# Down-projection by seven products of quarters (Strassen's kind), with running sums in PSUM, and a new order of all work

## The chip, the cores and the metric

One core of a Trainium2 chip runs the kernel. The metric is the device time of one execution, in microseconds. TensorE (PE) multiplies matrices from SBUF into PSUM, which has eight banks; VectorE (DVE) and ScalarE (ACT) can read PSUM; GpSimd (POOL) cannot, and it also issues DMAs, as SyncE (SP) does.

## The reference

A recurrent attention (decay per head) is followed by a normalised, gated feed-forward layer without biases. Cut to what matters:

```python
batch, n_heads, seq, head_dim = 4, 8, 768, 64      # 3072 tokens, d_model 512, d_ff 1536
for t in range(S):
    state = gamma * state + k_t (outer) v_t        # per batch and head
    y[t] = scale * q_t @ state
x = y as (B*S, H*D)
xn = x / sqrt(mean(x*x) + 1e-6) * rms_g
out = (silu(xn @ w_gate) * (xn @ w_val)) @ w_out   # float32 out
```

The last product is the down-projection: 3072 x 1536 by 1536 x 512.

## The kernel before

The 768 positions are cut into six chunks c of 128; with the four batches b a chunk has 512 tokens. For each (c, b) the attention computes masked scores (A, then M0 and M1 on VectorE write am), the output y (Y, in PSUM), the state update (K, U, B), the sum of squares (S, ScalarE), the reciprocal root (R, GpSimd), the normalised rows xn (N, VectorE) and their transpose xnT (X and XE on engines for chunks 0 and 1, a transposing DMA from SP later). Inputs come through L (Lq, Lk, Lv; @P is GpSimd's queue, which casts to bf16 on the way, @S is SP's, in float32), are cast or scaled by Ck, Cq and V, and transposed by Tq/Tk with copies Eq/Ek (chunks 0 and 1) or by DMA (tq, tk). J and D make decayed keys for chunks 0 and 1.

The feed-forward layer works on a chunk. Its 1536 inner columns are 12 slices n of 128. `g.c.n0.n1.b0.b1` and `v...` multiply slices of w_gate and w_val by xnT into a bank each (L549: four matmuls of 128x128 by 128x512 for a slice with all four batches), `s` is Silu on ScalarE (L559), `h` multiplies both on VectorE into the activations hT (L567). The down-projection `d.c.b.n0.n1` (L574) has, for each batch, 12 matmuls of a 128x128 slice of hT, held as weights, by 128x512 of w_out; `o` copies the bank out (L146, a helper for all copies), `st` stores it (L587). The last tile of the last chunk, (5, 3), is done by `e` in three pieces of 192, 192 and 128 columns (L596), so that the last copy and store are small. hT is a ring of two tiles of 12 slices, o_sb a ring of four.

All instructions stand in an order written out by hand in the string ORDER: each word names a function, its arguments, after `/` the PSUM banks, after `@` the engine. Every engine runs its own instructions in this order and waits by semaphores for others. The weights arrive by GpSimd DMAs (wg.n0.n1, wv.n0.n1, wo.n0.n1) placed among its other work. H and hot are filler matmuls on a constant, whose result nobody reads (L240, L234).

The functions that the diff touches are printed here.

Of the kernel before, what the change touches and what calls it, by code (L numbers as in the profile page):

```python
# [9 lines left out]
F32 = mybir.dt.float32  # L10
BF16 = mybir.dt.bfloat16
# [6 lines left out]
H.8/3 yt Lk.0.2@S ident Ck.0.2@D vd Lk.1.1@S iota Tk.0.2/0 rms.1@S D.0.2@D Lk.0.0@P Lq.0.1@P H.3/1 Tk.0.0/2  # L18
H.1/1 Tq.0.1/7 Ek.0.0@D mk1 hot.3/1 J.0.0/3 D.0.0@D mk0 Lq.0.0@P Lk.0.1@P Tq.0.0/6 Lq.0.2@P Eq.0.1@A Eq.0.0@A
Tk.0.1/5 Ek.0.1@A Ek.0.2@D yd Lk.0.3@P H.1/1 Tq.0.2/4 tab Lq.0.3@P Eq.0.2@D hot.2/0 A.0.0/5017 M0.0.0 G/2 M1.0.0  # L20
Tq.0.3/6 Lv.0.0@P M0.0.1 GE@A Tk.0.3/3 Eq.0.3@A Lv.0.1@P M1.0.1 Lv.0.2@P Lv.0.3@P wg.0.2 Y.0.0/4 wv.0.2 A.0.2/21
wg.2.4 M1.0.2 Ek.0.3@A Lq.1.1@P H.3/0 A.0.3/61 S.0.0 M0.0.2 H.1/0 Y.0.2/3 K.0.0/0 J.0.1/5 M1.0.3 R.0.0 S.0.2
N.0.0 M0.0.3 Y.0.1/1 H.1/2 X.0.0/4 J.0.3/7 wv.2.4 S.0.1 XE.0.0@D U.0.0@A R.0.2 R.0.1 Ck.1.1@A N.0.2 B.0.0 H.2/2
Y.0.3/0 g.0.0.2.0.1/2 K.0.2/6 S.0.3 s.0.0.2.0.1 N.0.1 U.0.2@A wg.4.6 X.0.2/4 R.0.3 XE.0.2@D D.0.1@D
v.0.0.2.0.1/3 X.0.1/2 wv.4.6 causal XE.0.1@A Lk.1.2@P v.0.0.2.2.3/4 wg.6.9 Lq.1.2@P wv.6.9 h.0.0.2.0.1
g.0.0.2.2.3/6 D.0.3@D Lq.1.0@P g.0.0.2.1.2/5 g.0.2.3.0.3/3 s.0.0.2.2.3 h.0.0.2.2.3 s.0.0.2.1.2 g.0.3.4.0.3/6
N.0.3 v.0.0.2.1.2/4 D.1.1@D Tq.1.1/5 Lk.1.0@P Tk.1.1/0 X.0.3/7 Eq.1.1@D K.0.1/2 wg.9.12 v.0.3.4.0.3/1 Lv.1.1@P
s.0.3.4.0.3 XE.0.3@A g.0.0.4.3.4/6 s.0.2.3.0.3 h.0.0.2.1.2 g.0.4.6.3.4/4 wv.9.12 g.0.4.5.0.3/7 v.0.4.6.3.4/5
v.0.2.3.0.3/3 U.0.1@D s.0.4.6.3.4 Ek.1.1@A h.0.3.4.0.3 g.0.5.6.0.3/0 s.0.4.5.0.3 h.0.4.6.3.4 mc.0@P mc.1@P
v.0.4.5.0.3/5 v.0.0.4.3.4/7 h.0.2.3.0.3 Tk.1.2/1 g.0.6.7.0.4/4 Ek.1.2@A Lv.1.2@P h.0.4.5.0.3 g.0.7.8.0.4/2  # L30
Lv.1.0@P wo.0.4 Tq.1.2/1 s.0.5.6.0.3 s.0.7.8.0.4 Eq.1.2@D B.0.1 g.0.8.9.0.4/3 A.1.2/51 v.0.5.6.0.3/0 M1.1.2
wo.4.8 wo.8.12 s.0.0.4.3.4 v.0.7.8.0.4/2 h.0.0.4.3.4 h.0.5.6.0.3 h.0.7.8.0.4 Lk.1.3@P D.1.2@P Lk.2.0@S
v.0.6.7.0.4/7 Tk.1.0/0 M0.1.2 Lk.2.3@S Tq.1.0/6 v.0.8.9.0.4/1 s.0.6.7.0.4 Ek.1.0@A Eq.1.0@D h.0.6.7.0.4
s.0.8.9.0.4 Lq.2.1@S A.1.0/6042 M0.1.1 M1.1.0 B.0.2 M1.1.1 g.0.11.12.0.4/3 g.0.9.10.0.4/5 g.0.10.11.0.4/4
s.0.11.12.0.4 K.1.1/3 Y.1.1/0 s.0.10.11.0.4 h.0.8.9.0.4 S.1.1 U.1.1@D M0.1.0 v.0.9.10.0.4/2 v.0.10.11.0.4/3
R.1.1 v.0.11.12.0.4/4 s.0.9.10.0.4 K.0.3/7 h.0.9.10.0.4 D.1.0@P U.0.3@A Y.1.2/2 S.1.2 h.0.10.11.0.4 Y.1.0/3
N.1.1 h.0.11.12.0.4 Lq.1.3@P S.1.0 B.0.3 Lq.2.0@S Lk.2.1@S K.1.0/7 X.1.1/5 R.1.2 K.1.2/1 U.1.2@D d.0.3.0.4/0
N.1.2 R.1.0 N.1.0 d.0.0.0.4/6 XE.1.1@D d.0.1.0.4/4 d.0.2.0.4/2 X.1.0/5 d.0.3.4.8 X.1.2/1 d.0.0.4.8 Lv.1.3@P
d.0.1.4.8 XE.1.2@D d.0.1.8.12 U.1.0@D XE.1.0@A B.1.1 g.1.0.1.0.3/7 Tk.1.3/5 g.1.1.2.0.3/3 d.0.3.8.12 Tq.1.3/1
o.0.1@D Eq.1.3@D d.0.0.8.12 s.1.1.2.0.3 Ek.1.3@A o.0.3@A A.1.3/13 M1.1.3 Ck.2.0@A M0.1.3 tk.2.0 v.1.1.2.0.3/0  # L40
d.0.2.4.8 o.0.0@A Y.1.3/3 h.1.1.2.0.3 v.1.0.1.0.3/6 Ck.2.3@D S.1.3 R.1.3 Cq.2.1@D g.1.3.4.0.3/1 v.1.2.3.0.3/4
# [24 lines left out]
d.2.2.0.12/1 R.3.3 K.3.2/4 N.3.0 S.3.2 N.3.3 d.2.1.0.10/2 d.2.1.10.12 XE.3.0@S Lq.5.2@S R.3.2 N.3.2 Ck.5.2@D
XE.3.2@S d.2.3.0.12/3 U.3.3@D XE.3.3@S U.3.2@D Lk.4.2@S o.2.2@D Lq.4.2@S Lv.5.3@S U.3.0@D d.2.0.0.10/4 tk.4.0
# [36 lines left out]
def kernel(  # L104
# [43 lines left out]
    def flat(x):  # L148
        return x.rearrange("p h d -> p (h d)")
# [485 lines left out]
```

## Time and profile before

| | |
|---|---|
| time, median of 3 runs | 235.12 us (234.45 to 295.99) |
| the profiled execution | span 233.6 us, 4637 instructions |
| mean granted TensorE clock | 0.993 |
| gate and value products, busy | 70.0 and 71.2 us, 344 matmuls each |
| down-projection, busy | 63.5 us in 276 matmuls of 512 columns, and 36 narrower ones |
| filler matmuls H | 8.5 us in 20 |
| memory traffic | 28.31 MB read, 6.29 MB written, 148 GB/s |

The profile comes from one execution. Its times are from the span's start; "busy" is the time in which an engine had an instruction of the group running, and since matmuls are pipelined and their ends modelled, the mean of one matmul in a group is longer than its share of a stream. "PEld" is the load of the stationary operand, beside PE.

### The profile page before, as it was taken

The numbers are of one execution on the slowest core, as the hardware profiler recorded it, in microseconds if no ns is written. First come the engines' busy times: TensorE is split into PE (matmuls) and PEld (weight loads), VectorE is DVE, ScalarE is ACT, GpSimd is POOL, SyncE is SP. The second block draws the span as 40 slices with busy tenths as digits, with TensorE's granted clock in tenths as the row PEclk, the third lists the DMA queues.
The fourth block names the chain that finished last, engine by engine and source line by source line (L and its number), as shares of the span: only waits on it lengthen the run. The fifth ranks groups of instructions, "written<-read, shape, count | busy, mean of one in ns | idle before, by whom it ended". The sixth has DMA issues, their size and how long they took to land.

```text
span 233.6 us, 4637 instructions
## 1 busy us (share of the span) xinstructions
PE 227.6 (97%) x1771; PEld 120.8 (52%) x1771; DVE 130.4 (56%) x241; ACT 96.1 (41%) x231; POOL 89.7 (38%) x163
## 2 busy tenths in 40 slices
PE   8799999999999999999999999999999999999994
PEld 2458855645545655445554444554455444444444
DVE  6479639753662965628975239866367532323320
ACT  7658433514337231464731346553265332232202
POOL 8958998550544555030273741247003100000000
PEclk9979999999999999999999999999999999999999
DMA  7999999999798888999988899968511400020222
GB/s 126 147 180 123 127 179 184 205 145 215 133 206 214 171 194 140 262 218 221 235 173 146 179 221 206 198 149 142 148 61 27 112 0 0 3 90 9 83 89 93
DMA packets 105353, 33.61 MB, mean 144 GB/s; under 512 B 94449, under 2 KB 102385, under 8 KB 105330
## 3 DMA queue, kind: packets, MB, share of 16 engines
q1 hardware_dynamic: 81858, 25.70, 50.2%
q0 software_dynamic: 23472, 7.60, 30.1%
q8 instruction: 14, 0.23, 0.4%
q14 instruction: 9, 0.07, 0.1%
HBM read 28.31 MB, written 6.29 MB: 148 GB/s over the span
## 4 chain that ended last, share of the span: by engine, by line
PE 89%; DMA 4%; POOL 2%; ACT 2%; DVE 1%; issue 0%; SPq 0%; POOLq 0%; DVEq 0%; ACTq 0%
PE v_ps L549 27%; PE g_ps L549 27%; PE o_ps L574 21%; PE a_ps L403 3%; DMA kb<-in_k_dram 3%; PE y_ps L441 2%; PE kv_ps L526 2%; PE y_ps L445 2%; DMA out_dram<-o_sb 1%; PE o_ps L596 1%; PE hot_ps L240 1%; PE t_ps L366 1%; PE t_ps L371 1%; PE xt_ps L495 1%; ACT xsq L455 1%; ACT xsq L458 1%
## 5 line engine op out<-in xcount | busy, mean ns | idle before, releaser
L567 DVE TENSOR_TENSOR hT<-sg,v_ps 128x512 bf16<-128x512 bf16 (+2 forms) x76 | 48.7, 656 | 47.8 <-PE v_ps L549 34.8
L549 PE MATMUL v_ps<-xnT,wv_b 128*128 128x512 bf16 (+2 forms) x344 | 71.2, 345 | 0.1
L559 ACT ACTIVATE sg<-g_ps 128x512 bf16<-128x512 f32 (+2 forms) x76 | 42.1, 575 | 70.6 <-PE g_ps L549 68.1
L549 PE MATMUL g_ps<-xnT,wg_b 128*128 128x512 bf16 (+2 forms) x344 | 70.0, 344 | 0.0
L574 PE MATMUL o_ps<-wo_b,hT 128*128 128x512 bf16 x276 | 63.5, 379 | 0.0
L549 PEld LDWEIGHTS <-wg_b 128*128 128x128 bf16 x344 | 30.4, 98 | 29.3
L549 PEld LDWEIGHTS <-wv_b 128*128 128x128 bf16 x344 | 30.2, 98 | 28.9 <-DVE am L426 0.6
L574 PEld LDWEIGHTS <-hT 128*128 128x128 bf16 x276 | 26.3, 98 | 29.1
L468 POOL TENSOR_SCALAR ms<-ssq 128x1 f32<-128x1 f32 x24 | 4.6, 190 | 59.1 <-ACT xsq L458 58.4
L426 DVE TENSOR_TENSOR am<-a_ps,causal 128x512 bf16<-128x512 f32 x32 | 20.6, 685 | 7.8 <-PE a_ps L403 7.5
L339 POOL TENSOR_TENSOR qb<-qf,ydec 128x512 bf16<-128x512 f32 x13 | 14.0, 1074 | 25.2 <-DMA qf<-in_q_dram 24.9
L146 ACT COPY o_sb<-o_ps 128x512 f32<-128x512 f32 (+1 forms) x16 | 8.8, 552 | 29.7 <-PE o_ps L574 23.1
L458 ACT ACTIVATE xsq<-y_ps 128x512 f32<-128x512 f32 x22 | 13.2, 599 | 18.9 <-PE y_ps L445 13.7
L482 DVE SCALAR_TENSOR_TENSOR xn<-y_ps,rstd,g_bc 128x512 bf16<-128x512 f32 x22 | 16.3, 748 | 4.3 <-POOL rstd L470 3.0
L146 DVE COPY o_sb<-o_ps 128x512 f32<-128x512 f32 (+1 forms) x10 | 6.4, 648 | 18.1 <-PE o_ps L574 12.2
L541 POOL CAST st_b<-st_f 64x256 bf16<-64x256 f32 x40 | 15.9, 398 | 1.3
L470 POOL TENSOR_TENSOR rstd<-ms,mhalf 128x1 f32<-128x1 f32 x24 | 13.3, 552 | 2.0
L534 DVE TENSOR_TENSOR st_f<-st_f,kv_ps 128x512 f32<-128x512 f32 x16 | 10.8, 684 | 5.2 <-PE kv_ps L526 4.6
L356 ACT ACTIVATE vp<-vf,vdec 128x64 bf16<-128x64 f32 x48 | 12.2, 343 | 0.0
L426 DVE TENSOR_TENSOR am<-a_ps,mask 128x512 bf16<-128x512 f32 x16 | 10.4, 686 | 2.5 <-PE a_ps L403 2.3
L240 PE MATMUL hot_ps<-one 128*128 128x512 bf16 x20 | 8.5, 547 | 1.1 <-DVE one L153 1.1
L441 PEld LDWEIGHTS <-am 128*128 128x128 bf16 x176 | 7.8, 99 | 3.1 <-issue 0.3
(99 smaller groups left out, 174.8 us busy)
## 6 DMA issues: line engine op xcount, KB each, us to landing
out_dram<-o_sb SPq DMA_DIRECT2D x23, 256.0 KB, 2.4
kf<-in_k_dram SPq DMA_DIRECT2D x18, 256.0 KB, 3.8
qf<-in_q_dram SPq DMA_DIRECT2D x16, 256.0 KB, 3.9
vf<-in_v_dram SPq DMA_DIRECT2D x16, 256.0 KB, 3.9
wo_b<-in_moe_w_out_dram POOLq DMA_DIRECT2D x3, 512.0 KB, 12.2
qb<-in_q_dram POOLq DMA_DIRECT2D x8, 128.0 KB, 6.6
vp<-in_v_dram POOLq DMA_DIRECT2D x8, 128.0 KB, 6.5
kb<-in_k_dram POOLq DMA_DIRECT2D x6, 128.0 KB, 5.9
```

The source lines that it names most:

```text
L146: (e.copy if e is ACT else e.tensor_copy)(out, in_)
L339: e.tensor_tensor(out=u["qb"], in0=u["qf"], in1=ydec[:, c, :, None].to_broadcast([128, H, D]), op=ALU.mult)
L426: DVE.tensor_tensor(out=u["am"][:, i], in0=u["a"][i], in1=m, op=ALU.mult)
L441: nc.tensor.matmul(y[:, h, :], u["am"][:, h % 2, h // 2, :], u["vp"][:, h, :], start=h == 0, stop=c == 0 and h == H - 1, skip_group_check= ...
L458: ACT.activation(xsq, flat(u["y"]), AF.Square, accum_out=u["ssq"])
L470: POOL.tensor_tensor(out=u["rstd"], in0=ms, in1=mhalf, op=ALU.pow)
L482: DVE.scalar_tensor_tensor(out=u["xn"], in0=flat(u["y"]), scalar=u["rstd"], in1=g_bc, op0=ALU.mult, op1=ALU.mult)
L541: POOL.tensor_copy(st_b[b][r, :, i * 64:i * 64 + 64], st_f[b][r, :, i * 64:i * 64 + 64])
L549: nc.tensor.matmul(p[:, (n - n0) * m:(n - n0 + 1) * m], W[w][0][:, s, n * 128:(n + 1) * 128], xnT[c][:, s, b0 * C:b1 * C], start=s == 0, s ...
L559: ACT.activation(sg[:, :cols], done["wg", c, n0, b0][:, :cols], AF.Silu)
L567: DVE.tensor_tensor(out=hT[c][:, n0:n1, b0 * C:b1 * C], in0=sg, in1=p, op=ALU.mult)
L574: nc.tensor.matmul(o_ps[c, b], hT[c][:, n, b * C:(b + 1) * C], wo_b[:, n, :], start=n == 0, stop=n == NFF - 1)
```

## The change

Chunk 0 keeps the old down-projection (`d`, `o`, `st`). For chunks 1 to 5 the product hT by w_out is cut into quarters: tokens into two halves of 256 (batches 0, 1 and 2, 3), the inner dimension into two halves (of every four slices, the first two and the last two), the output columns into two halves of 256. Instead of eight products of quarters there are seven, by Winograd's form of Strassen's method. With A11, A12, A21, A22 for the quarters of the activations (first index: half of the tokens) and B for those of w_out:

- w1 = B12 - B11, w2 = B22 - w1, w3 = B22 - B12 (in place of B12), w4 = B21 - w2: once, three on VectorE, w3 on GpSimd, 1536 bf16 elements in each partition.
- z1 = A21 + A22, z2 = z1 - A11, z3 = A11 - A21 (in place of A21), z4 = A12 - z2: for each chunk and each third r of the slices, 512 bf16 elements in each partition: 60 instructions, 33 on VectorE and 27 on GpSimd.
- Products: 1 = A11 B11, 2 = A12 B21, 3 = z4 B22, 4 = A22 w4, 5 = z1 w1, 6 = z2 w2, 7 = z3 w3. Each is 12 matmuls of 128x128 by 128x256 into one bank, which holds two blocks of 128 tokens.
- Bank a takes 1, 6, 7 and 4 as a running sum. After 1, 6 and 7 a copy q leaves it (q1, q6, q7), mostly by ScalarE; after 4 it is the third quarter, C21, copied by r4. Bank b takes 2, and r1 = b + q1 (VectorE) is C11. Bank c takes 5, r2 = c + q7 is C22; then 3 is added into it, and r3 = c + q6 is C12. s1 to s4 store the quarters, 256 KB each.

Word for word in the new order: `a1.c.r0.r1`, `a6`, `a7`, `a4`, `b2`, `c5`, `c3` are the products.

Buffers change with it: hT is a ring of five tiles of four slices; z shares a ring of 12 with kd; w shares three wide tiles with the masks of chunks 0 and 1; the results share o_sb, five tiles, with two tiles of the start; xsq is one bf16 tile. The pieces `e` are gone. The whole ORDER is another one. Its start, the part around the first sums, and its end:

```diff
+Lk.0.2@S rms.1@S Lk.1.1@S Lq.0.3@P Lk.0.0@P Lk.0.1@P Lq.0.0@P H.8/0 H.1/1 Lq.0.1@P iota hot.3/2 mk1 ident yt pick
+Lq.0.2@P Tq.0.3/3 Tk.0.0/4 Ck.0.2@D vd Ck.1.1@A D.0.2@D H.1/5 Lk.0.3@P Lq.1.2@P Tk.0.1/6 Lv.0.0@P Eq.0.3@D Lv.0.1@P
+Tk.0.2/7 Ek.0.2@D Ek.0.0@A Tq.0.0/0 Lk.1.0@P Ek.0.1@A J.0.0/1 D.0.0@D Tq.0.1/2 Eq.0.0@A Tk.1.1/5 Lv.0.2@P Eq.0.1@A
+J.0.1/4 D.0.1@D Ek.1.1@D Tq.0.2/3 A.0.0/6701 M1.0.0 M1.0.1 Eq.0.2@A Tk.0.3/2 mk0 M0.0.1 Ek.0.3@A G/4 M0.0.0 Lk.1.2@P
+Tq.1.2/5 A.0.3/37 M1.0.3 A.0.2/12 Lv.0.3@P M0.0.2 Lk.1.3@P Eq.1.2@D Y.0.1/0 S.0.1 wg.4.6 Lq.1.3@P K.0.0/6 U.0.0@A
+K.0.1/7 Y.0.0/1 hot.2/6 U.0.1@A GE@A M0.0.3 M1.0.2 J.0.3/5 R.0.1 wg.6.9 H.1/7 S.0.0 R.0.0 Y.0.3/6 N.0.1 N.0.0 wv.6.9
+S.0.3 Tk.1.0/2 Tk.1.2/4 Y.0.2/3 H.2/7 Tk.1.3/0 S.0.2 Ek.1.2@A Ek.1.0@D Ek.1.3@A R.0.3 H.3/7 D.0.3@D X.0.1/1 K.0.2/2
+XE.0.1@A N.0.3 R.0.2 K.0.3/4 U.0.3@A wv.4.6 Lq.1.1@P X.0.0/7 A.1.2/50 N.0.2 X.0.3/6 XE.0.3@D XE.0.0@A Tq.1.3/1 X.0.2/4
+XE.0.2@D yd tab U.0.2@A g.0.4.6.3.4/3 g.0.6.7.0.4/7 s.0.4.6.3.4 wg.0.2 Eq.1.3@D g.0.5.6.0.3/6 g.0.7.8.0.4/4
...
+h.1.11.12.0.4 Y.2.1/5 S.2.1 v.1.8.9.0.4/4 R.2.1 N.2.1 s.1.10.11.0.4 d.0.3.8.12 v.1.10.11.0.4/2 A.3.0/3601 Lk.3.2@S
+o.0.3@A h.1.8.9.0.4 Cq.3.3@D V.3.0@P h.1.10.11.0.4 a1.1.0.3/5 M1.3.0 q1.1@D B.2.0 XE.2.0@S K.3.0/7 U.3.0@D B.2.1
+z1.1.2@D M0.3.1 b2.1.0.3/4 XE.2.2@S XE.2.1@S g.2.3.4.0.4/2 v.2.3.4.0.4/6 s.2.3.4.0.4 Lv.3.2@S z2.1.0@D g.2.10.11.0.4/7
...
+Lk.5.3@S Ck.5.3@P P.4.2/451630 B.4.2 N.4.1 q1.2@A M1.4.2 M0.4.3 M0.4.2 a6.2.0.3 M1.4.3 Y.4.0/7 V.5.2@A K.4.3/5
...
+c5.4.0.3/5 h.5.10.11.0.4 z4.5.0@D z1.5.2@D z3.5.2@D r2.4 s3.3@S s2.4@S z4.4.1@D b2.5.0.2/1 a6.5.0.2 b2.5.2.3 r1.5
+z2.5.2@P a6.5.2.3 q6.5@A s1.5@S c5.5.0.2/0 a7.5.0.2 c5.5.2.3 s2.3@S a7.5.2.3 z4.5.2@D z4.4.0@D c3.4.0.3 q7.5@A r2.5
+s2.5@S a4.5.0.2 H.1/7 r3.4 s3.4@S a4.5.2.3.0 z4.5.1@P c3.5.0.2 r4.5.0@A a4.5.2.3.1 s4.5.0@S r4.5.1@A s4.5.1@S c3.5.2.3
+r3.5 s3.5@S H.3/4
```

The code, cut to its core:

```diff
+    HB, OB, KD, SN = 5, 5, 12, 3
+    def wide(name):
+        return sb.tile([128, 1024], F32, name=name, tag="wide", bufs=3)
...
-            hT[c] = ring([128, NFF, GT], BF16, "hT", 2)
+            hT[c, r] = ring([128, 4, GT], BF16, "hT", HB)
...
+    wo_q = wo_b.rearrange("p (r j i) m -> p r j i m", j=2, i=2)
+    def block(j, m):
+        return wo_q[:, :, j, :, m * HM:(m + 1) * HM]
+    def quarter(c, r, i, j):
+        return hT[c, r][:, (J0, J1)[j], (LO, HI)[i]]
+    def zsum(i, e, c, r, x, a, b, how):
+        if x is None:
+            x = sb.tile([128, 2, GT // 2], BF16, name="z", tag="kd", bufs=KD)
+        e.tensor_tensor(out=x, in0=a, in1=b, op=how)
+        done["z", i, c, r] = x
...
+    def product(x, i, bk, c, r0, r1, p=None):
+        first = i in (1, 2, 5) and r0 == 0
+        if first:
+            done[x, c] = bank(bk[0], [128, 2, HM], F32, x)
+        for q in (0, 1) if p is None else (p,):
+            for r in range(r0, r1):
+                for k in (0, 1):
+                    nc.tensor.matmul(done[x, c][:, q], left(i, c, r)[:, k, q * C:q * C + C], right(i)[:, r, k],
+                                     start=first and q == r == k == 0, stop=r == 2 and k == 1, skip_group_check=True)
+    def keep(i, e, c):
+        done["q", i, c] = ring([128, 2, HM], F32, "sn", SN)
+        copy(e, done["q", i, c], done["a", c])
+    QUARTER = {1: ("b", 1, 0, 0), 2: ("c", 7, 1, 1), 3: ("c", 6, 0, 1), 4: ("a", None, 1, 0)}
+    def result(i, e, c, p=None):
...
+            DVE.tensor_tensor(out=done["r", i, c][:, s], in0=done[x, c][:, s], in1=done["q", q, c][:, s], op=ALU.add)
+    def store(i, e, c, p=None):
+        _, _, t0, m = QUARTER[i]
+        s = slice(0, 2) if p is None else slice(p, p + 1)
+        e.dma_start(out=out_v[c][s.start + 2 * t0:s.stop + 2 * t0, :, m * HM:(m + 1) * HM]
+                    .rearrange("b p m -> p b m"), in_=done["r", i, c][:, s])
```

More of the change, by code (lines that the diff above doesn't have):

```diff
@@ L192 @@
     g_bc = const.tile([128, DM], F32, name="g_bc")
-    g_row = const.tile([1, DM], F32, name="g_row")
+    g_row = spare([128, DM], F32, "g_row")[0:1]
     ones = const.tile([1, 128], F32, name="ones")
@@ L584, in st, with o @@
[L584 to L597 removed]
+    def o(e, bk, c, b):
+        done["o", c, b] = ring([128, DM], F32, "o_sb", OB)
+        copy(e, done["o", c, b], o_ps[c, b])
```

226 lines of the change are left out of this document (121 added, 105 removed).

## The prediction

> **What bounds the kernel now.** I read the page's first two parts, then the shares of the chain that ended last.
>
> ```profile
> span 233.6 us, 4637 instructions
> PE 227.6 (97%) x1771; PEld 120.8 (52%) x1771; DVE 130.4 (56%) x241; ACT 96.1 (41%) x231; POOL 89.7 (38%) x163
> PEclk9979999999999999999999999999999999999999
> PE 89%; DMA 4%; POOL 2%; ACT 2%; DVE 1%; issue 0%; SPq 0%; POOLq 0%; DVEq 0%; ACTq 0%
> ```
>
> TensorE is busy 97% of the span, the chain runs through it for 89%, and the clock is full but for one early slice. A busy row does not yet say that it works at its rate, so I took the chain in order of time (columns: start, length, what), where a run of matmuls shows its spacing.
>
> ```profile
> 24.20 0.45 PE t_ps L371 x8
> 53.94 0.65 PE g_ps L549 x4
> 75.41 0.55 PE a_ps L403 x16
> 88.32 2.59 PE o_ps L574 x12
> 227.81 2.66 PE o_ps L596 x36
> 230.50 0.32 ACT o_sb L146
> ```
>
> Per matmul: 0.45 / 8 = 56 ns for 128 columns, 0.65 / 4 = 163 for 384, 2.59 / 12 = 216 for 512. That is a straight line, 0.416 ns a column and about 3 ns on top. TensorE is bound by columns streamed, and only fewer columns, or less waiting, shorten it. Where does it not stream? At the start:
>
> ```profile
> 5.00:19.38 14.38, 12.88 (x218) 7.66 (x217) 9.47 (x16) 10.02 (x25) 10.61 (x18) 0.88 1.56 164
> 19.38 0.61 PE L549 MATMUL g_ps<-xnT,wg_b 128*128 128x128 bf16 x8
> 61.00:131.00 70.00, 70.00 (x513) 36.40 (x512) 43.40 (x71) 28.33 (x73) 29.30 (x51) 1.00 0.94 199
> L240 PE MATMUL hot_ps<-one 128*128 128x512 bf16 x20 | 8.5, 547 | 1.1 <-DVE one L153 1.1
> ```
>
> The stretches are: length, then busy time (count) of PE, PEld, DVE, ACT, POOL, then granted clock and DMA. The first gate product comes at 19.38; until then 20 wide filler matmuls stand in for work. Afterwards TensorE is full (70.00 of 70 from 61 to 131) while VectorE has 43.40 in 71 instructions there, 0.61 each. So after 19 us a saved column is a saved time, as long as no other engine fills up.
>
> **The products.** Chunks 1 to 5 used 48 matmuls of 512 columns each; the last chunk used 36 and the 36 narrow ones of L596. Before: 4 x 48 x 0.2158 + 36 x 0.2158 + 2.66 = 51.86 us. Now a chunk has seven products of 3 x 2 x 2 = 12 matmuls with 256 columns: 84 a chunk, 420 in all. No 256-column matmul is in the trace; the line gives 256 x 0.416 + 3 = 109 ns, between the rows of 128 and 384 columns. What could spoil it is the load of the stationary operand, of which there are now 420 for 240 (and 36):
>
> ```profile
> L574 PEld LDWEIGHTS <-hT 128*128 128x128 bf16 x276 | 26.3, 98 | 29.1
> ```
>
> One takes 98 ns, less than 109, and behind 128-column matmuls loads of this length keep a pitch of 56, so they overlap. Bounds: 109 and, if a load of 98 hid only half, 158. I take 109: 420 x 0.1092 = 45.89, a gain of **5.97 us**.
>
> A rule speaks against this split: the Trainium skill ("TensorE: Matmul & The Clock Gate", Back-to-back issue gap) gives 81 ns for 128 columns and 131 for 512 in streams of load and matmul, so about half of a wide matmul would be a fixed price. An estimate from that page, 98 ns for 256, would make the change 420 x 98 - 240 x 131 ns = 9.7 us dearer. The trace disagrees at both ends, with 56 and 216 ns.
>
> **What the other engines get.** Rows of the groups by shape (count, busy us and mean ns):
>
> ```profile
> L146 ACT COPY o_sb<-o_ps 128x512 f32<-128x512 f32 x14 | 8.2, 586 | 28.0 <-PE o_ps L574 23.1 <-DMA out_dram<-o_sb 4.8
> L146 DVE COPY o_sb<-o_ps 128x512 f32<-128x512 f32 x9 | 6.1, 687 | 14.6 <-PE o_ps L574 12.2 <-DMA out_dram<-o_sb 2.4
> L517 DVE TENSOR_TENSOR kd<-kb,vdec 128x512 bf16<-128x512 bf16 x3 | 2.1, 686 | 0.3 <-ACT vdec L259 0.3
> L146 DVE COPY xnT<-xt_ps 128x512 bf16<-128x512 bf16 x5 | 2.1, 422 | 2.1 <-PE xt_ps L495 2.1
> L517 POOL TENSOR_TENSOR kd<-kb,vdec 128x512 bf16<-128x512 bf16 x2 | 2.1, 1035 | 0.1
> 11.61 2.48 DVE L426 TENSOR_TENSOR am<-a_ps,mask 128x512 bf16<-128x512 f32 x4
> ```
>
> Removed: 22 of the 26 copies of o. Added: 15 sums r1 to r3 on VectorE, 15 mid copies q and 6 copies r4, mostly on ScalarE, where 586 each about equals the 16 copies that leave it. Further 60 sums z (33 on VectorE, 27 on GpSimd) and four sums w of three times the width. A z has 512 bf16 elements and two SBUF operands, which the trace shows only with a broadcast factor in another type (686); the bf16 copy's 422 is the other bound. I take 422, since nothing in a z is wider than bf16, and keep 686 for the range. GpSimd: 27 x 1.04 + 3.1 (w3) = 31 us on 89.7, free enough.
>
> VectorE must be judged by stage. Between the call z1.1.0 and the first product of chunk 3 the new order has 97 VectorE instructions beside 65 us of matmuls (the order's matmuls at the pitches above). Of these 15 (z and casts) cost 0.42, three w 1.2 each, and 79 cost 0.62, the pitch of the four masks in a row (2.48 / 4): 6.3 + 3.6 + 49.0 = 58.9 of 65, 91%; with z at the upper price 61.5. Before it was 43.40 of 70, 62%. TensorE is still the longer, so I cost all this at **nothing**, and TensorE's work is the cover: 6.1 us of room. When it is used up, the next late thing is a PSUM bank that VectorE has not emptied.
>
> **New waits.** After products 1, 6 and 7 a copy q must leave the bank before the next product adds into it; TensorE stands in order behind it, with every later matmul queued. A copy is 0.59 on ScalarE. The tightest covers are q1.2 (the attention call P.4.2, 0.77 us) and q6.5 (two thirds of c5.5, 8 x 0.109 = 0.87): zero, with 0.2 us to spare. Uncovered, 15 copies with some 0.1 around each would cost 15 x 0.7 = 11 us. The activations' ring is now five tiles of four slices, and the chunk before is read out ahead of the tile that reuses it: nothing. Chunk 0 keeps its 48 wide matmuls, which only move behind most of chunk 1's gates; SP issues 25 stores for 26, later, with transposes and loads in between, and the ring of five result tiles is the cover. Without it r waits on VectorE for a store, 2.4 us a time (row below), with h and U queued behind.
>
> **The start.** The new order puts first in TensorE's stream, ahead of the first gate product, three more xt transposes, three more K, six of chunk 1's transposes and one A: 12 groups of four at 56 ns and one of eight at 0.55 / 16 = 34 ns, 2.98 us. So it is level if that product starts at 19.38 + 2.98 = 22.36. VectorE must do 24 instructions before it, 18 x 0.62 + 6 x 0.42 + 0.5 = 14.2 us, from about 5.2 (five loads issued first on POOL, then the identity): 19.4 if it never idles, 24.3 with the 4.9 us idle that it had from 5.00 to 19.38 (14.38 - 9.47). I take 21.4, a gain of 1.0. On POOL's queue the first weights are moved behind fifteen loads of q, k and v, up from eleven, and the second behind sixteen:
>
> ```profile
> L312 POOL DMA_DIRECT2D qb<-in_q_dram x4 | 2.1, 542 | 0.0
> L314 POOL DMA_DIRECT2D vp<-in_v_dram x4 | 3.6, 946 | 0.0
> wg_b<-in_moe_w_gate_dram POOLq DMA_DIRECT2D x2, 384.0 KB, 8.3
> ```
>
> Seven short issues of 0.54, nine of 0.95 and the first weights, some 0.8, are 13.1 us; from about 1.2, with the identity between, the second weights are issued at about 15 and land 8.3 later, at 23, beside a gate product due at 22. Later weights have R, B and the masks of chunk 1 ahead of them and are due just as late. I charge 0.5 for all. Net **-0.5**, range -3.0 to +3.4. The clock's early dip (0.88) may move with it; that lies inside.
>
> **The end.** Before: a 192-column copy of 0.32 and a small store. Now r3.5, a full VectorE sum, 0.69, and a store of 256 KB:
>
> ```profile
> out_dram<-o_sb SPq DMA_DIRECT2D x23, 256.0 KB, 2.4
> out_dram<-o_sb SPq DMA_DIRECT2D x2, 96.0 KB, 1.7
> ```
>
> +0.37 + 0.7 = **+1.07**, and one filler among the last products, **+0.2**. The last fillers lie beside the store.
>
> **Sum.** 233.6 - 5.97 - 0.5 + 1.07 + 0.2 = 228.4 on the profiled execution. The median of the runs, 235.12, is 1.5 above it: **229.9**. From the terms, the start above all, 227 to 231.5, or 233.8 with its worst.
>
> **Rivals.**
>
> *VectorE fills up.* SBUF sums on VectorE and GpSimd may hold each other. From 125:
>
> ```profile
> 125.52 1.37 POOL L339 TENSOR_TENSOR qb<-qf,ydec 128x512 bf16<-128x512 f32 x1 [2.22 <-DMA qf<-in_q_dram]
> 125.31 0.68 DVE L358 TENSOR_TENSOR vp<-vf,vdec 128x512 bf16<-128x512 f32 x1
> L339 POOL TENSOR_TENSOR qb<-qf,ydec x13: 1037/1042/1372, 63.1 to 158.9; 128x512 bf16<-128x512 f32 x13
> ```
>
> The one qb that began under a VectorE product of two SBUF operands is the longest of 13, 1372 against a median of 1042. The Trainium skill ("SBUF — State Buffer", Who interferes with whom) has a rule for it: a VectorE instruction with two SBUF inputs and a GpSimd one that reads SBUF exclude each other, and whichever began second waits. The row agrees for the wait of GpSimd; no row here shows VectorE's.
>
> In the 65 us stretch 27 VectorE instructions (13 z, 3 w, 8 qb, 3 vp) have two SBUF operands. GpSimd was busy 29.30 of 70; 0.42 x half of 1.04 = 0.22 us a time, 27 x 0.22 = 5.9 of the 6.1 us of room. From 0.23 each it decides. With 0.4 TensorE waits 27 x 0.4 - 6.1 = 4.7, 234.6; from 0.59 the kernel is slower than 239.8, with 0.75 it comes to 244. For it: 91% is more than any stage had. Against: GpSimd's other instructions there are short. Chance 0.24: 0.13 under 239.8, 0.11 over.
>
> *The start is late*: weights and VectorE's idle time at their worst, 229.9 + 0.5 + 3.4 = 233.8. For: the queue above. Against: VectorE's idle time was partly waiting for the loads that now come first. 0.10.
>
> *Mid copies uncovered*: +11, 241; needs ScalarE late at each. 0.02.
>
> *A fixed price per matmul*: the 240 wide ones cost 51.9 us, so from 123 ns for 256 columns the gain is gone; at the 158 above, 229.9 + 420 x 0.049 = 250. The straight line speaks against it. 0.02.
>
> **Numbers.** About 2% (230.4 to 239.8) is what a measurement of this kernel tells from no change. The forecast has 0.62, of which 0.50 below 230.4 and 0.12 above. Faster 0.50; same 0.12 + 0.13 + 0.10 = 0.35; slower 0.11 + 0.04 = 0.15. The range 227 to 236 leaves out 0.15 of slower cases and the ends of others, about 0.2. The forecast's own range is 227 to 231.5.
>
> **What would show it.** Products: a row of 12 in 1.31 us in the chain; 1.9 or more refutes the rate. VectorE: z near 0.42 with TensorE at full length from 60 to 125; if instead TensorE waits for VectorE (am, hT or U) there, the rival holds. Start: first gate product near 21.4, no wait for wg_b or wv_b. End: chain closing with r, 0.69, and its store. The prediction is wrong if the stage from 60 to 125 loses more than the products save.

## The result, and the profile after

| | before | after |
|---|---|---|
| time, median | 234.78 us (three runs of 233.69 to 235.12, and a disturbed one of 295.99, which the ratio leaves out) | 240.08 us (four runs, 239.65 to 241.56) |
| ratio, 95% interval | | 1.0262 [1.0219, 1.0304], slower |
| the profiled execution | span 233.6 us | span 237.6 us, time 239.65 us |

229.9 was predicted, between 227 and 236: the time lies outside the range and on the other side. First the page of after: span, two engines, clock, use of the DMA engines in 40 slices, and the chain of waits by engine.

```profile
span 237.6 us, 5036 instructions
PE 223.1 (94%) x1927; PEld 137.3 (58%) x1927; DVE 159.9 (67%) x294; ACT 100.7 (42%) x243; POOL 118.4 (50%) x183
PEclk9799999999999999999999999999999999999999
DMA  6999999998988998989997795764014530010235
PE 61%; DMA 20%; DVE 6%; POOL 3%; ACT 3%; issue 3%; SPq 2%; ACTq 0%; POOLq 0%; DVEq 0%
```

TensorE is busy for 4.5 us less than before (223.1 for 227.6), as a change that saves columns should make it. But the span is 4.0 longer, so the time in which TensorE does nothing went from 233.6 - 227.6 = 6.0 to 237.6 - 223.1 = 14.5 us. The chain says where: 20% of it are now DMAs, 4% before. Those who read only that the work shrank would have expected a gain. Was the work itself done at the predicted rate? The chain of after, in order of time:

```profile
102.46 1.31 PE a L656 x12
...
233.13 0.45 PE c L656 x4
...
233.61 0.69 DVE r L679
```

Twelve matmuls in 1.31 us are 109 ns each, exactly the forecast, and the end is r and its store, as forecast. So the loss is waiting, and the next question is when. The stretches (columns as in the prediction), after:

```profile
61.00:131.00 70.00, 66.40 (x509) 37.48 (x508) 55.20 (x87) 32.28 (x83) 32.91 (x48) 1.00 0.98 185
0.00:94.47 94.47, 84.95 (x883) 51.83 (x883) 66.33 (x138) 44.07 (x101) 64.20 (x109) 0.98 1.25 171
94.47:237.50 143.03, 138.17 (x1044) 85.51 (x1044) 93.58 (x157) 56.63 (x142) 54.16 (x76) 1.00 0.53 122
```

TensorE, full from 61 to 131 before, now has holes of 3.6 us there. The last two rows are cut at the first gate product of chunk 2, which I call the date. Before, the same cut:

```profile
0.00:94.82 94.82, 92.21 (x904) 53.86 (x905) 60.00 (x128) 43.68 (x101) 59.87 (x104) 0.98 1.16 171
94.82:233.50 138.68, 135.41 (x868) 66.93 (x866) 70.40 (x114) 52.40 (x131) 29.79 (x59) 1.00 0.57 126
```

The date is the same, 94.82 and 94.47, but by then TensorE has done 92.21 us of work before and 84.95 after. The 7.3 us that are missing have to be done behind it: in the old order all 48 wide matmuls of chunk 1's down-projection stand ahead of the date, in the new one only two of its seven products (24 narrow matmuls); chunk 0's 48 are ahead of it in both. The missing work eats what the products save, and the rest of the span is 143.03 instead of 138.68. Up to the date TensorE is idle for 9.5 us instead of 2.6: 1.7 more than before ahead of the first gate product, 1.8 from there to 61 us and 3.4 from 61 to the date, two stretches in which it was never idle before. What sets the date? The chain of after again, three pieces of it, and then the one piece before the date in the kernel before:

```profile
58.92 9.07 DMA qf<-in_q_dram
...
68.08 0.70 DVE qb L350
...
75.63 5.29 DMA kT<-kb
...
80.96 0.40 PE a_ps L414 x8
...
91.23 3.20 DMA xnT<-xn
...
94.47 1.04 PE g_ps L560 x4
```

```profile
94.28 0.54 PE o_ps L574 x2
94.82 1.73 PE g_ps L549 x8
```

Before, TensorE came to the gate product from its own stream. After, it came from an input: a load of q that took 9.07 us, a transposing DMA, another. The waits of TensorE in after (line, what it waited for, us in total, times, longest) name the same:

```profile
PE o_ps L589 <- DVE hT L582: 1.9, 1, 1.9
PE t_ps L377 <- DMA qb<-in_q_dram: 1.7, 1, 1.7
PE y_ps L452 <- DMA vp<-in_v_dram: 1.4, 2, 0.8
...
PE a_ps L414 <- DMA kT<-kb: 1.0, 1, 1.0
...
PE v_ps L560 <- DMA xnT<-xn: 0.6, 1, 0.6
```

The first looks like VectorE, and isn't; the second is at the start, 4.8 to 6.4 us. VectorE's timeline shows h standing in order behind a cast of q that waited 3.10 us for its load:

```profile
68.08 0.69 DVE L350 TENSOR_TENSOR qb<-qf,ydec 128x512 bf16<-128x512 f32 x1 [3.10 <-DMA qf<-in_q_dram]
68.69 1.28 DVE L582 TENSOR_TENSOR hT<-sg,v_ps 128x512 bf16<-128x512 bf16 x2
```

The new order needs inputs sooner. The tile of these loads in after and then in before (shortest, median and longest issue in ns, first and last start; then the time to landing):

```profile
L325 SPq DMA_DIRECT2D qf<-in_q_dram x16: 373/581/1093, 42.9 to 137.1; - x16
DMA to landing us min/median/max: 3.3/4.4/9.1
```

```profile
L314 SPq DMA_DIRECT2D qf<-in_q_dram x16: 572/580/1457, 51.8 to 153.2; - x16
DMA to landing us min/median/max: 3.3/3.9/5.0
```

The first load of q from SP goes out 9 us earlier, the last 16 earlier. (In both kernels all loads of chunk 2 wait, by a dependency written into `load`, for the load wo.8.12 of w_out; SP waited 48.0 us for it before and 40.6 after.) They go into DMA engines that are as full as before, 7 to 9 tenths in every slice of the first half but the first. The row of before, beside that of after above:

```profile
DMA  7999999999798888999988899968511400020222
```

And the two stretches up to the date moved at the same rate, 171 GB/s: 171 x 94.5 us are 16.2 MB in both, though before 1 MB of it was four stores, and after it has no store and three loads more. That is the theory I tested: *the change asks for about the same bytes with 7 us less work to cover them, and the inputs, not TensorE, now set the date.* The rivals: VectorE is held up by GpSimd's sums, or simply has too much; or the seven products themselves cost it.

### The profile page after: what moved, and what is told of

It is laid out like the page before. It is cut to its first block, busy times and chain, and to the rows that moved or that the text cites. A ratio compares the mean times of both kernels' runs of the same rounds, so it can differ in the third digit from the quotient of the medians.

```text
span 237.6 us, 5036 instructions
## 1 busy us (share of the span) xinstructions
PE 223.1 (94%) x1927; PEld 137.3 (58%) x1927; DVE 159.9 (67%) x294; ACT 100.7 (42%) x243; POOL 118.4 (50%) x183
## 4 chain that ended last, share of the span: by engine, by line
PE 61%; DMA 20%; DVE 6%; POOL 3%; ACT 3%; issue 3%; SPq 2%; ACTq 0%; POOLq 0%; DVEq 0%
PE v_ps L560 19%; PE g_ps L560 16%; PE a L656 9%; PE c L656 6%; DMA qf<-in_q_dram 4%; DMA vf<-in_v_dram 3%; DMA xnT<-xn 3%; DMA vp<-in_v_dram 3%; DMA wv_b<-in_moe_w_val_dram 3%; DMA kb<-in_k_dram 2%; DMA kT<-kb 2%; PE b L656 2%; SPq L398 2%; PE y_ps L452 2%; PE a_ps L414 1%
## 5 line engine op out<-in xcount | busy, mean ns | idle before, releaser
L656 PEld LDWEIGHTS <-hT 128*128 128x128 bf16 x240 | 23.3, 98 | 5.3
L629 POOL TENSOR_TENSOR z<-hT 128x512 bf16<-128x512 bf16 x6 | 7.0, 1172 | 31.6 <-DVE hT L582 31.5
L552 POOL CAST st_b<-st_f 64x256 bf16<-64x256 f32 x40 | 18.0, 450 | 7.9 <-PE y_ps L456 6.4
L656 PEld LDWEIGHTS <-z 128*128 128x128 bf16 x180 | 17.5, 98 | 3.3
L469 ACT ACTIVATE xsq<-y_ps 128x512 bf16<-128x512 f32 x22 | 13.2, 598 | 11.5 <-PE y_ps L456 9.9
L656 PE MATMUL a<-wo_b,hT 128*128 128x256 bf16 x120 | 14.9, 273 | 0.0
L589 PE MATMUL o_ps<-wo_b,hT 128*128 128x512 bf16 x48 | 11.3, 379 | 1.9 <-DVE hT L582 1.9
L629 POOL TENSOR_TENSOR z<-z,hT 128x512 bf16<-128x512 bf16 x6 | 7.4, 1235 | 11.0 <-DVE z L629 10.9
L350 DVE TENSOR_TENSOR qb<-qf,ydec 128x512 bf16<-128x512 f32 x12 | 10.0, 831 | 4.2 <-DMA qf<-in_q_dram 4.2
L148 ACT COPY sn<-a 128x512 f32<-128x512 f32 x10 | 5.9, 586 | 14.0 <-PE a L656 14.0
```

The source lines that it names most:

```text
L469: ACT.activation(xsq, flat(u["y"]), AF.Square, accum_out=u["ssq"])
L552: POOL.tensor_copy(st_b[b][r, :, i * 64:i * 64 + 64], st_f[b][r, :, i * 64:i * 64 + 64])
L589: nc.tensor.matmul(o_ps[c, b], hT[c, n // 4][:, n % 4, b * C:(b + 1) * C], wo_b[:, n, :], start=n == 0, stop=n == NFF - 1)
L629: e.tensor_tensor(out=x, in0=a, in1=b, op=how)
L656: nc.tensor.matmul(done[x, c][:, q], left(i, c, r)[:, k, q * C:q * C + C], right(i)[:, r, k], start=first and q == r == k == 0, stop=r == ...
```

## The experiments

"The date" is the first gate product of chunk 2, "the rest" the span less the date. The kernel before was run on the same chip each time, at medians of 233.6 to 234.1; ratios are to it, with their 95% interval.

**The new order without the products.** Each chunk has the plain down-projection, four tiles put where products 4, 2, 5 and 3 were, and no sums.

```diff
-a1.1.0.3/5 M1.3.0 q1.1@D B.2.0 ... z1.1.2@D M0.3.1 b2.1.0.3/4
+M1.3.0 B.2.0 ... M0.3.1 d.1.1.0.12/4
```

> The new order with the old arithmetic: chunks 1 to 5 are again 4 x 12 products of 512 columns, put where a4, b2, c5 and c3 stand, with their four copies and stores; no sums z and w, no copies q; the activations' ring gets nine tiles. TensorE's work goes back up by 6.0 us (45.9 to 51.9). Theory A, that the new order itself puts inputs late (the waits at 39, 48, 67, 76 and 80 us of the changed kernel, all of which stand before the first product): the waiting of 17.9 us stays, 240.1 + 6.0 = 246, not under 243. Theory B, that the sums z and w fill VectorE and lock the port for GpSimd: the waiting falls back to 8.1 us as before the change, about 236, not over 239.

251.58 us (249.75 to 253.66), 1.0727 [1.0645, 1.0809], longer than either theory said. The date is 94.30, although no sum and no product exists; the rest is 153.7. So the order alone costs about 17 us with these places of the plain tiles (my choice, other places may do better). The kernel with the products is 11 us faster, of which 6.0 would be columns by the forecast; what makes up the other 5 was not separated. The products aren't what makes the date late.

**No sums.** All z and w are gone; the products read fixed slices of a weight in place of z, and raw blocks of w_out in place of w.

```diff
-        return done["z", {3: 4, 5: 1, 6: 2, 7: 3}[i], c, r]
+        return quarter(...) if i in (1, 2, 4) else wg_b[:, 0:2, 0:256]
-        return done["w", {4: 4, 5: 1, 6: 2, 7: 3}[i]]
+        return block(*{4: (1, 0), 5: (0, 1), 6: (1, 1), 7: (0, 1)}[i])
```

> The changed kernel without the 60 sums z and the four sums w; the products that used them read fixed slices of wg_b on the left and raw blocks of wo_b on the right, so that TensorE has the same matmuls at the same places and the output of chunks 1 to 5 is not the reference's. Theory A (order and inputs): 239 to 240.5, within 1 us of the changed kernel, and the waits at 39, 48 and 67 us stay. Theory B (sums): VectorE loses some 20 us and GpSimd 31 us of work, the waiting of TensorE between 60 and 165 us (9 us) goes for the most part, 233 to 235.

241.39 us (238.28 to 243.78), 1.0239 [1.0172, 1.0306], for 1.0262 with the sums. VectorE was busy 142.1 us for 159.9 and GpSimd 82.5 for 118.4, and it changed nothing that can be measured: date 93.50, rest 142.8. The rival of VectorE and the SBUF port falls here.

**One cast later, then inputs in the order of use.** In the first, VectorE's cast Cq.2.0, behind which h had waited, goes behind two groups of products. In the second, three loads also change places: v of chunk 1 (1.2 and 1.3 swapped, 1.0 earlier) and q 2.0 before k 3.0.

```diff
-Cq.2.2@P Cq.2.0@D g.1.4.5.0.4/4 ... v.1.2.3.0.3/4 tq.2.0
+Cq.2.2@P g.1.4.5.0.4/4 ... v.1.2.3.0.3/4 Cq.2.0@D tq.2.0
```
```diff
-... Lv.1.2@P ... Lv.1.3@P ... wv.9.12 ... Lv.1.0@P ... Lk.3.0@S ... Lq.2.0@S
+... Lv.1.3@P ... Lv.1.2@P ... wv.9.12 Lv.1.0@P ... Lq.2.0@S ... Lk.3.0@S
```

> One instruction of the changed kernel moved: VectorE's scaling of the q rows of chunk 2, row 0 (qb, L350), which waits for a load that lands at 68 us, stands behind the two products h (L582) that follow it in VectorE's order, so that these no longer queue behind it and the PSUM bank of the second d comes free. Theory A: the wait of 2.0 us at 67 us goes; what follows is again late by the transposing DMA at 76 and 80 us, which hang on the same load and do not move, so that 0.5 to 2.0 us are won, 238 to 239.6. Theory B: nothing, 240.

> As the run with one cast moved, and besides three loads earlier: v of chunk 1 row 3 changes places with row 2 on GpSimd's queue, v of row 0 is issued right after the last weights of wv (39 us instead of 42.6), and on SyncE's queue the q load of chunk 2 row 0 changes places with the k load of chunk 3 row 0, which stands six loads ahead of it. Sums and products as they are. Theory A: the waits at 39 (0.94), 48 (0.80) and 67 us (2.02) go, and those at 76 and 80 (1.6 together) in part: 235.5 to 237.5. Theory B: 239.5 to 240.5. A third theory, that the DMA engines (over 0.9 busy from 6 to 115 us) deliver no faster whatever the order of issue: the waits move to other inputs, 239 to 240.5.

243.07 us, 1.0395 [1.0373, 1.0416], and 241.04, 1.0284 [1.0223, 1.0344]: no gain, and the first is slower than the change (1.0262 [1.0219, 1.0304]). In each kernel the waits that the edit aimed at went away, and others came: in the first, TensorE waited 2.9 us for xnT at the date (95.57), in the second 2.2 us for a qT (date 94.14). A wait that was taken away in this stretch, short of inputs, came back at the next input. I had expected the single waits to add up; they don't. After either of these longer waits the granted clock was 0.50 for some 3 us (last section); in the first kernel that lies behind the date, where 2.85 us at half the clock cost 1.4 of the 1.9 us by which its rest (144.93) is longer.

**SP's queue.** As the second, and five loads of chunk 3 behind the last transpose of chunk 2, so that chunk 2 would have the DMA engines.

```diff
-... Lk.3.0@S ... Lk.3.1@S ... Lq.3.0@S ... Lq.3.1@S ... tk.2.1 A.2.0/5204 Cq.3.1@D tk.3.0 Lv.3.0@S
+... tk.2.1 Lk.3.0@S Lq.3.0@S Lk.3.1@S Lv.3.0@S Lq.3.1@S A.2.0/5204
```

> The changed kernel with its inputs reordered once more: as in the run with three loads earlier, and on SyncE's queue five loads of chunk 3 (k of rows 0 and 1, q of rows 0 and 1, v of row 0) stand behind the last transposing DMA of chunk 2 instead of among its loads and transposes; in their place q of chunk 2 row 0 and v of rows 1 and 0 are issued earlier; the casts and transposes of chunk 3 rows 0 and 1 follow later. Sums and products as they are. Theory A1 (SyncE's order: transposes stand behind loads whose buffers are not free): the waits between 67 and 81 us (1.6 + 2.0 in the changed kernel, 4 in the run with three loads earlier) shrink to under 1.5 us: 236 to 238. Theory A2 (the DMA engines cannot bring chunk 2 by 70 us in any order): within 1 us of the run with three loads earlier, 240 to 242, with the wait at the scores of chunk 2.

244.76 us, 1.0488 [1.0427, 1.0549], worse: date 99.73 in the profiled execution, the longest of its four. My own place for the cast Cq.3.1, ahead of its load on VectorE, was a new wait (TensorE waited 2.7 us for VectorE's st_f behind it). A miss, with a granted clock of 0.91 up to the date: it doesn't separate the theories.

**Fewer bytes.** This is the test that does. The loads wo.0.4 and wo.4.8 (1 MB written to SBUF) are left out; GpSimd sets those rows of w_out to zero, 1.83 us each.

```diff
-... v.1.3.4.0.3/6 wo.0.4 h.1.3.4.0.3 wo.4.8
+... wv.9.12 wz.0.4 ... Lv.1.0@P wz.4.8
+    def wz(e, bk, n0, n1):
+        POOL.memset(wo_b[:, n0:n1, :], 0.0)
```

> The changed kernel without two of the three loads of wo (1 MB that is issued at 55.9 to 57.5 us); the rows of wo that they bring are set to zero by GpSimd at about 40 and 44 us, so that the output isn't the reference's; all else as it is. Theory A2 (the DMA engines are full, and q of chunk 2 row 0 takes 9.07 us to land because 1 MB of wo travels with it): q of chunk 2 row 0 lands in 4 to 5 us, so 4 us earlier, the wait of 2.0 us at 67 us goes and those at 76 and 80 us as well: 236 to 237.5. Theory A1 (SyncE's queue order): the wait at 67 goes, but the transposes keep their pace and the waits come back at the scores: 239 to 240.5.

236.09 us, 1.0099 [1.0065, 1.0133]. The chain and the stretches:

```profile
87.65 2.97 DMA xnT<-xn
...
90.66 1.04 PE g_ps L564 x4
```

```profile
0.00:90.66 90.66, 85.16 (x884) 52.15 (x884) 66.73 (x139) 44.15 (x101) 66.18 (x109) 0.98 1.17 166
90.66:233.70 143.04, 138.26 (x1044) 85.47 (x1044) 93.87 (x156) 56.59 (x142) 53.24 (x75) 1.00 0.54 122
```

The date came 3.8 us earlier, the rest stayed at 143.04 (143.03 in after) and the span is 3.8 shorter. Nothing but two loads was taken away (two memsets of GpSimd came in), TensorE did the same work up to the date (85.16 for 84.95), and the worst landing of a q load on SP's queue went from 9.1 to 6.1 us:

```profile
DMA to landing us min/median/max: 3.5/4.5/6.1
```

The weights left out were on GpSimd's queue, the load is on SP's. The Trainium skill ("DMA: Bandwidth & Descriptors", Issuing engines are not separate DMA queues) says that all issuers' transfers run on the same 16 engines and interleave; these two rows agree.

If the date is set by inputs only in the new order, the kernel before should not gain from the same cut. There VectorE sets the rows to zero.

> The kernel before (old order, plain down-projection) without the same two loads of wo (1 MB); its rows of wo are set to zero by VectorE, two instructions, so that the output isn't the reference's. If the old order has its inputs on time (theory A2: its TensorE waits for no load between 20 and 150 us), the 1 MB is worth nothing here: 233 to 234.5, the first gate product of chunk 2 stays at 94.8 us within 0.5 us. If the DMA engines held the old order too, it gains like the changed kernel did (4 us): 229.5 to 230.5.

235.6 us, 1.0073 [1.0044, 1.0103]; date 95.12, no gain, rather a loss of 1.7 us, above the range expected. A wait of 0.9 us at 35 us stands behind VectorE's second instruction that sets the rows to zero; the rest stays unexplained. Its chain enters the date from TensorE's own stream:

```profile
94.58 0.54 PE o_ps L574 x2
95.12 1.08 PE g_ps L549 x5
```

So the same megabyte is worth 3.8 us of span in the new order and brings nothing in the old one.

**The same bytes earlier.** The two loads of w_out are kept, but issued at 39 and 44 us, before the stretch in which they disturbed.

```diff
-... v.1.3.4.0.3/6 wo.0.4 h.1.3.4.0.3 wo.4.8
+... wv.9.12 wo.0.4 ... Lv.1.0@P wo.4.8
```

> The changed kernel with its second and third load of wo issued at about 39 and 44 us, where GpSimd's queue idles, instead of 55.9 and 57.5 us; the same bytes, nothing else moved. If the DMA engines are simply full from 6 to 115 us (theory A2), the 1 MB only changes places with the first loads of chunk 2, which start at 42.9 us: q of chunk 2 row 0 lands earlier, other inputs later, 238.5 to 241. If what counts is that 1 MB meets the last q load (theory A3), the waits at 67 to 80 us (3.7 us) go: 236 to 237.5, as without the 1 MB (236.1).

241.63 us, 1.0332 [1.0296, 1.0368]; date 96.46. The waits from 67 to 80 are gone, and one of 3.66 us at 49 took their place. Its chain:

```profile
43.26 9.40 DMA vp<-in_v_dram
...
52.70 0.61 PE y_ps L452 x8
```

A load of v, half as large in SBUF as that of q, now takes 9.40 us (median 6.0 in after). The bytes have to go somewhere ahead of the date. (Behind that wait TensorE had a granted clock of 0.50 for another 3 us, so not all of the later date is the inputs'.) Up to their date all kernels with all loads and the new order moved 16.1 to 16.2 MB (rate times length), at 162 to 173 GB/s; the highest rate of any kernel here up to the date was 175. At that, 16.15 MB take 92.3 us, which gives an estimate of how much the same loads at that rate could win: about 2 of the 4.0 us lost. It is no bound: ten of SP's 24 loads that the order puts ahead of the date are for chunks 3 and 4, and whether the date needs all these bytes wasn't shown.

**More room for the inputs.** a1.1, q1.1 and b2.1 move behind the first gate and value products of chunk 2.

```diff
-a1.1.0.3/5 M1.3.0 q1.1@D B.2.0 ... M0.3.1 b2.1.0.3/4 ... g.2.3.4.0.4/2 v.2.3.4.0.4/6
+M1.3.0 B.2.0 ... M0.3.1 ... g.2.3.4.0.4/2 v.2.3.4.0.4/6 a1.1.0.3/5 q1.1@D b2.1.0.3/4
```

> The changed kernel with its first two products of chunk 1 and the copy between them (24 matmuls, 2.6 us) moved from just before the first gate and value products of chunk 2 to just behind them; nothing added or taken away. If the date of that gate product is fixed by the inputs' chain (loads, scores, rows xnT) and not by TensorE's work (theory A4: what counts is the work that is left after it), TensorE's wait for xnT grows from 0.5 to about 3 us, the gate product stays at 94 to 94.5 us, and the whole is 2.0 to 2.6 us longer than the changed kernel on the same chip. If TensorE's work sets the date, the gate product comes 2.6 us earlier and the time is that of the changed kernel, within 0.5 us.

> The changed kernel as it is, on the same chip as the two beside it, as their reference: 239.5 to 241.5, first gate product of chunk 2 at 94 to 95 us.

244.7 us, 1.0451 [1.0405, 1.0497], beside the change itself again at 240.73, 1.0315 [1.0246, 1.0385]. Date 95.72 and 94.25: 2.6 us of work less stood ahead of the first one, and it came no earlier; TensorE waited longer. The stretch up to the date (84.95 of work in after) and the timeline of TensorE:

```profile
0.00:95.72 95.72, 83.09 (x850) 50.59 (x860) 67.14 (x138) 43.86 (x101) 65.84 (x110) 1.00 1.18 169
```

```profile
95.72 1.89 PE L560 MATMUL g_ps<-xnT,wg_b 128*128 128x512 bf16 x4 [4.17 <-DMA xnT<-xn]
```

Work that was moved behind the date was lost to it. The rest is 147.2 for 143.4, longer by the 2.6 us and by a low clock (last section).

**The old order with products.** Twice I put the products of chunks 1 to 4 into the order of before.

> The other half of the change alone: the order of the kernel before, in which the 48 wide products of each of chunks 1 to 4 are replaced, where they stood, by the seven products with their sums z, copies q and results r; the four sums w stand at about 55 to 65 us; chunk 0 and the last chunk stay as they were before; the ring of activations has six tiles, that of z ten, that of q two. TensorE's work falls by 192 x 0.2158 - 336 x 0.1092 = 4.7 us. Theory A (the new order costs, the products gain): 234.1 - 4.7 = 229.4, not over 231. Theory D (the wide products were also the cover of the next chunk's attention, from its scores to its transposed rows xnT, and with fewer columns there TensorE waits for xnT at the first gate product of each chunk, up to 1.2 us a chunk and more where sums z stand in VectorE's order ahead of the masks): 232 to 236, with waits before g_ps at about 88, 122, 160 us.

> The order of the kernel before with the products in chunks 1 to 4, placed anew. Against the first attempt (259.9): two stores of chunk 0 stand earlier on SyncE's queue, so that the copy of r4 no longer waits 7 us for its result tile; all four w and 36 of the 48 z go to GpSimd, so that VectorE's masks don't queue behind them; the running sums stand in banks that are free by then. TensorE's work is 4.7 us less than before. Theory A (with inputs as early as before, the products gain what they save): 229 to 231. Theory D (the wide products were the cover of the next chunk's attention, 75 to 87 us, and with fewer columns TensorE waits before each chunk's first gate product): 232 to 236, with those waits in the trace. Over 238 would mean that GpSimd's sums (16 x 1.15 us a chunk) hold the attention's own steps on GpSimd (R, B, V) or, at the same time, VectorE's.

259.93 us (255.74 to 260.59, without an interval), and 265.59 with 1.1325 [1.1261, 1.1388]. Both lost far more than they could gain. Two of TensorE's waits in the second, the longest in total and the longest single one:

```profile
PE a L666 <- POOL hT L639: 4.5, 6, 0.9
...
PE y_ps L450 <- POOL vp L367: 3.0, 1, 3.0
```

Here the products waited for GpSimd's sums, and the next chunk's attention for a vp that stood in order behind such sums; in the first the longest entries were VectorE's st_f (5.3 us in three waits) and a copy r of ScalarE (3.4). These are my places, and show only that sums and copies need places of their own beside the next chunk's attention, not that none would do.

**The products alone, in one chunk.** So I asked where a chunk has no attention beside it: chunk 4. First the order and the arithmetic of before in the new code with its smaller rings, then the same with seven products in chunk 4.

```diff
-d.4.0.0.12 o.4.0 ... st.4.0@S
+a1.4.0.3 q1.4@A b2.4.0.3 r1.4 a6.4.0.3 q6.4@A ... z1.4.0@P ... s4.4@S
```

> The order and the plain down-projection of the kernel before, in the changed kernel's code: six activation tiles of four slices for two of twelve, one bf16 scratch for the squares, the masks in the shared wide buffers; no product, no sum. Reference for the run beside it. No theory expects a cost: 233.5 to 234.5, ratio 0.998 to 1.003.

> The same with the seven products in chunk 4 alone, where GpSimd has 3 us of work in 35 and the DMA engines are 0.2 busy, and no attention of a later chunk but the last rows of chunk 5 is beside it; the twelve z on GpSimd, the four w on VectorE from about 183 us. TensorE has 48 x 0.2158 - 84 x 0.1092 = 1.19 us less. Theory E (the products gain what they save wherever the stage is bound by TensorE's columns; what the changed kernel lost is the stage before 94 us): 1.0 to 1.2 us less than the run beside it, 232.4 to 233.3. Theory F (the products cost as much as they save in any place, by sums, copies and PSUM banks): within 0.5 us of it, or more than it.

233.49 us (twelve runs, 0.9991 [0.9966, 1.0016]) and **232.63** (twelve runs, 0.9961 [0.9946, 0.9976]): a gain of 0.4%, under the 2% that counts as faster here, but with an interval clear of 1; it is the fastest kernel here. The products should save 48 x 0.2158 - 84 x 0.1092 = 1.19 us; the medians differ by 0.86, the profiled spans (231.8 and 230.6) by 1.2. With runs of 233.12 to 235.65 and 232.51 to 233.46 the difference to 1.19 is within the noise. One new wait can be seen in its chain:

```profile
201.12 1.32 PE a L664 x12
...
202.47 0.03 ACT sn L144
202.50 0.46 issue
202.95 0.61 ACT sg L566
...
203.59 0.70 DVE hT L578
...
204.33 1.02 PE v_ps L556 x4
```

ScalarE's copy q7 stands ahead of a Silu, which holds h, the bank and the next value product: 0.17 us of idle TensorE (204.33 less the end of the eight gate matmuls, 202.44 + 8 x 0.216 = 204.17). So the arithmetic is worth about what was forecast when TensorE is fed, by a direct test, and the copy leaves a small price.

## Why the prediction was wrong

**Products, right.** 109 ns a matmul in the row above; 1.19 us a chunk forecast, 0.86 measured with about that much noise. Neither of the rival prices per matmul (123 and 158 ns) holds. The rule of the Trainium skill ("TensorE: Matmul & The Clock Gate", Back-to-back issue gap) that would have made the change 9.7 us dearer gives 131 ns for 512 columns and, by an estimate from it, 98 for 256. The traces have 216 (12 in 2.59) and 109 (12 in 1.31): they don't agree, and the measurement decides.

**Inputs: the step that failed.** It is the sentence in "What the other engines get" that costs the whole work from chunk 1's sums to chunk 3 at nothing because "TensorE's work is the cover", with 6.1 us of room. It counts what VectorE has to do, and takes for granted that its operands are there. In the same way "Chunk 0 keeps its 48 wide matmuls, which only move" and the place of chunk 1's products were costed at nothing. The new order's loads of q, k, v and the transposes were priced only at the start. I worked out TensorE's work ahead of the first gate product, but not ahead of later inputs. Done with the pitches of the prediction and without the fillers, the order would have shown about 58.5 us of TensorE's work ahead of chunk 2's first scores instead of 62.9, and 71.3 instead of 81.0 ahead of chunk 3's (estimates): the same loads due 4 to 10 us sooner. The page of before had the other half: DMA engines at 7 to 9 tenths over that whole stretch (row above). The cover was 7.3 us short where the date is, and the runs show that the date doesn't follow the work: 95.72 with 2.6 us less of it, 90.66 with as much work and a megabyte less, 94.30 without any sum or product. The cover that was costed at nothing cost 6.9 us of new idle time up to the date, 1.7 of it at the start, and 1.6 behind it.

**VectorE fills up, 0.24: fell.** It would have made 234.6 to 244 by sums that hold each other. The time lies in there, but for another reason: without any sums it is the same. VectorE's one wait of over 0.2 us in TensorE's list stands behind an input.

**z at 0.42, w at 1.2: right, and without effect.** A z on VectorE had medians of 417 to 419 ns (rows in the last section); the three w took from 0.95 to 1.73. GpSimd's z took 1.15, not 1.04.

**Start: too hopeful.** The first gate product came at 22.94, later than the level 22.36 and the 21.4 taken, and the wait for wv_b was 0.30 of the 0.5 charged; so the term was some +0.9 instead of -0.5. That it had no effect is argued, not tested: it lies ahead of a date that the inputs set.

**Mid copies, end, rings: right.** TensorE's list of waits has none for a copy q or a ring; in the kernel with one chunk a copy, through the Silu behind it, cost 0.17.

**The criterion was set too narrow.** "The prediction is wrong if the stage from 60 to 125 loses more than the products save": from 61 to 131 TensorE lost 3.6 us, less than the 6.0 saved. The loss shows when it is counted from the start: 7.3 us less work up to the date.

Still open: whether the new order can be remade so that chunk 1's products stand ahead of the date. Their sums would have to be done before 90 us, and PSUM has banks for it only if others leave; I didn't try it. Nor was it tried to let chunk 2's loads go before wo.8.12 has landed, or whether the rate of the DMA engines or the order of the loads is the tighter limit. In the first experiment the rest is 153.7 - 138.7 = 15.0 us longer than before; its stretch gives 8.6 of them to TensorE's work (144.05 for 135.41, and some matmul records are missing there) and 6.4 to idle time (9.65 for 3.27). The end, where the tiles stand at my places, makes 2.4 of the idle time.

## What to carry to other kernels

Before costing moved work at nothing because TensorE is full, mark a later step that needs an input (here a chunk's first gate product), count the work ahead of it in both orders, and compare with the bytes that must land by then: here the DMA engines were full up to it, the date stayed, and the work moved behind it was lost. Test it by taking bytes away in both kernels; a wait that disappears while the date stays was never the cause. And try an arithmetic saving first in the one stage that has nothing else beside it.

## What the runs showed of the hardware

**The clock fell after waits of about 2 us.** The change itself, run a second time, had a wait of 2.09 us at the same place where its first profile has 1.86. The timeline of TensorE and a stretch, second run, then both of the first:

```profile
68.93 3.02 PE L589 MATMUL o_ps<-wo_b,hT 128*128 128x512 bf16 x8 [2.09 <-DVE hT L582]
```

```profile
70.00:72.00 2.00, 2.00 (x8) 0.83 (x7) 1.97 (x5) 0.00 (x0) 0.58 (x1) 0.50 0.50 113
```

```profile
69.42 1.89 PE L589 MATMUL o_ps<-wo_b,hT 128*128 128x512 bf16 x8 [1.86 <-DVE hT L582]
```

```profile
70.00:72.00 2.00, 2.00 (x14) 1.01 (x12) 1.97 (x5) 0.00 (x0) 0.09 (x1) 1.00 0.51 116
```

The same eight matmuls took 3.02 us after the longer wait and 1.89 after the shorter; the low clock lasted some 3.4 us, so it cost about 1.7 beside the wait. The kernel with later products had the same at 0.50 after its 4.17 us, and so had, behind the start, every wait of TensorE from 2.09 us up in the kept traces; of those between 1.8 and 2.0 two of 1.98 had it, and 1.86, 1.87 and 1.88 hadn't. The Trainium skill ("TensorE: Matmul & The Clock Gate", HAM oscillation — how this bites in real kernels) gives gaps of more than about 3.4 us as the rule; here 2.09 was enough, and the measurement decides.

**VectorE does wait for GpSimd's sums.** The trace of before showed only GpSimd held. The tile z in after, two of VectorE's three kinds (ns: shortest, median, longest):

```profile
L629 DVE TENSOR_TENSOR z<-hT x9: 411/419/691, 70.8 to 224.0; 128x512 bf16<-128x512 bf16 x9
L629 DVE TENSOR_TENSOR z<-z,hT x9: 415/419/1181, 95.3 to 208.8; 128x512 bf16<-128x512 bf16 x9
```

In the second kernel of the old order, where GpSimd's sums z3 (written in place, tile hT) run at the same time, the z on VectorE has a median of 1259:

```profile
L639 DVE TENSOR_TENSOR z<-hT,z x9: 416/1259/1376, 97.3 to 182.4; 128x512 bf16<-128x512 bf16 x9
L639 POOL TENSOR_TENSOR hT<-hT x12: 1142/1156/1398, 93.3 to 230.5; 128x512 bf16<-128x512 bf16 x12
```

Of GpSimd's sums in this row the longest took 1398 for a median of 1156, VectorE's took mostly three times their usual 419: the effect of the rival exists, but it didn't set the time of this change.
